# The first load of the output projection's weights in two unequal parts: 112 rows, then eight rows twice

## The chip, the core and the metric

The kernel runs on one core of one Trainium2 chip, alone. The metric is the device time of one execution in microseconds (us), the median of three runs. All data is float32.

## What is computed

One decoding step of a transformer block for a batch of two, one new position each: layer normalisation, attention over a cache of 8192 positions with 16 heads of 256, an output projection, a second layer normalisation and a gated feed-forward without a nonlinearity. Cut to what matters:

```python
B, D, H, Sk, Dh, F = 2, 448, 16, 8192, 256, 1792
n = layernorm(x)                                   # (B, 1, D)
q = (n @ wq) split into H heads of Dh
p = softmax(q . k_cache * Dh ** -0.5)              # k_cache, v_cache: (B, H, Sk, Dh)
o = p . v_cache                                    # (B, H, 1, Dh)
h = x + o (heads side by side) @ wo                # wo: (H * Dh, D)
m = layernorm(h)
out = h + ((m @ w_gate) * (m @ w_up)) @ w_down     # w_gate, w_up: (D, F); w_down: (F, D)
```

The two caches are 512 MiB of the 561 MB that the core reads.

## The kernel before, in words

The host lays every weight and every piece of the cache out as 128 rows, one for each partition of the on-chip memory, so that each load is a plain copy of 128 contiguous rows.

- All loads are issued from SyncE's queue (SP), in the order of the program, and run as one stream. The first is `wq_t` (line 107). Then come, for each of the 32 pairs of head and batch, one load of keys (`load_k`, line 98, one buffer in the pool `kbuf`) and one of values (`load_v`, line 103, two buffers in `vbuf`), each of 128 rows of 65,536 bytes.
- TensorE and VectorE share the scores (`scores`, lines 253 to 278), ScalarE makes the exponentials (line 324), VectorE multiplies and sums the values (lines 343 to 352). The key buffer comes free when the scores of a pair are done, so the load after it waits for VectorE's line 261 and TensorE's lines 269 and 275.
- After the 32 pairs the remaining weights reuse the same buffers. `wo_t`, the weights of the output projection, takes the key buffer; `gu_t` (gate and up) and `wd_t` (down) take the two value buffers. `wo_t` comes in three loads, cut by heads at `WO_CUTS = (8, 14)`: heads 0 to 7 (7168 columns, 28,672 bytes in each row), heads 8 to 13 and heads 14 and 15. Gate comes in two loads, up in three and down in six (lines 364 to 370), the later ones ever smaller.
- Line 395 (`project_out`) multiplies by `wo_t`, line 201 by `gu_t`, line 462 by `wd_t`. Line 476 and its partner on ScalarE copy the result, and line 477 stores two rows of it.
- The framework gives each load the next of eight completion semaphores (DMAHW0 to DMAHW7 in the rows further down). A load that takes a semaphore waits for the load that had it eight places earlier, unless the queue has waited for that already.

The function is one long stretch of code without loops on the chip; what the change touches are lines 357 to 359:

Of the kernel before, what the change touches and what calls it, by code (L numbers as in the profile page):

```python
# [15 lines left out]
P = 128  # L16
# [8 lines left out]
WO = 2 * D  # L25
# [34 lines left out]
def tile_decode_block(  # L60
# [24 lines left out]
    nc = tc.nc  # L85
# [270 lines left out]

    wo_t = kbuf.tile([P, H * WO], F32, tag="k", align_bytes=512, name="wo_t")
    for a, z in zip((0,) + WO_CUTS, WO_CUTS + (H,)):
        nc.sync.dma_start(wo_t[:, a * WO : z * WO], wo[:, a * WO : z * WO])
    gu_t = vbuf.tile([P, 2, WF], F32, tag="v", align_bytes=512, name="gu_t")  # L360
    wg_t, wu_t = gu_t[:, 0], gu_t[:, 1]
    wd_t = vbuf.tile([P, NF * D], F32, tag="v", align_bytes=512, name="wd_t")
# [51 lines left out]
    for m in range(DC + 1):  # L414
        at = min(m, DC - 1)
        rows = slice(0, P) if m < DC - 1 else slice((m - at) * HALF, (m - at + 1) * HALF)
# [128 lines left out]
```

## Time and profile before

| | |
|---|---|
| time, median of 3 runs | 1303.92 us (1303.78 to 1304.15) |
| profiled execution, first to last instruction (span) | 1302.1 us |
| difference between the two | 1.8 us |
| read from HBM | 561.19 MB, 431 GB/s over the span |
| VectorE busy | 1075.6 us (83%) |
| TensorE busy (matmul) | 340.6 us (26%) |
| the three loads of `wo_t` | 3584, 2688 and 896 KB, 16.5, 22.5 and 24.2 us from issue to landing |

A profile page of one execution gives, for each engine, its busy time; the span in 40 equal slices with the busy share of the 16 DMA engines and what they moved; the chain of work that ended last; and the costliest groups of instructions. A load's time to landing includes its place in the stream: the loads ahead of it have to go through first. KB are of 1024 bytes, MB and GB of 10^6 and 10^9.

### The profile page before, as it was taken

The numbers are of one execution on the slowest core, as the hardware profiler recorded it, in microseconds if no ns is written. First come the engines' busy times: TensorE is split into PE (matmuls) and PEld (weight loads), VectorE is DVE, ScalarE is ACT, GpSimd is POOL, SyncE is SP. The second block draws the span as 40 slices with busy tenths as digits, with TensorE's granted clock in tenths as the row PEclk, the third lists the DMA queues.
The fourth block names the chain that finished last, engine by engine and source line by source line (L and its number), as shares of the span: only waits on it lengthen the run. The fifth ranks groups of instructions, "written<-read, shape, count | busy, mean of one in ns | idle before, by whom it ended". The sixth has DMA issues, their size and how long they took to land.

```text
span 1302.1 us, 5034 instructions
## 1 busy us (share of the span) xinstructions
PE 340.6 (26%) x2114; PEld 103.4 (8%) x2114; DVE 1075.6 (83%) x381; ACT 80.4 (6%) x111; POOL 2.2 (0%) x15
## 2 busy tenths in 40 slices
PE   2422112232202223211322311322311232221247
PEld 0100000000000000000000000000000000000013
DVE  0499879969987998899799879979987996987773
ACT  1100000000000000000000000000000000000000
POOL 0000000000000000000000000000000000000000
PEclk9866566666556666556666556666656666656668
DMA  9999999999999999999999999999999999999998
GB/s 419 419 449 421 447 423 445 425 443 427 439 429 441 425 441 427 437 428 437 433 435 433 434 435 435 435 433 437 431 439 431 437 429 435 433 433 433 433 425 358
DMA packets 11401, 561.50 MB, mean 431 GB/s; under 512 B 1266, under 2 KB 1652, under 8 KB 2292
## 3 DMA queue, kind: packets, MB, share of 16 engines
q1 hardware_dynamic: 11380, 561.20, 99.6%
q8 instruction: 16, 0.26, 0.1%
q14 instruction: 5, 0.04, 0.0%
HBM read 561.19 MB, written 0.00 MB: 431 GB/s over the span
## 4 chain that ended last, share of the span: by engine, by line
DMA 73%; PE 17%; DVE 10%; issue 1%; SPq 0%; DVEq 0%; ACT 0%; ACTq 0%
DMA k<-in_kc_dram 67%; PE s L269 13%; DVE k L261 6%; DMA v<-in_vc_dram 4%; PE s L275 3%; DVE v L350 3%; DMA wd_t<-in_wd_dram 2%; DVE k L256 1%; PE acc_ps L462 0%; SPq L366 0%; SPq L107 0%; PE u_ps L462 0%; SPq L98 0%; DVEq L256 0%; ACT tail L184 0%
## 5 line engine op out<-in xcount | busy, mean ns | idle before, releaser
L269 PE MATMUL s<-k,q 128*32 128x512 f32 x1632 | 248.3, 773 | 892.5 <-DMA k<-in_kc_dram 892.5
L346 DVE TENSOR_TENSOR v<-v,p 128x16384 f32<-128x16384 f32 x19 | 327.3, 17226 | 81.2 <-DMA v<-in_vc_dram 61.2
L347 DVE TENSOR_REDUCE oacc<-v 128x8 f32<-128x16384 f32 x19 | 327.2, 17220 | 0.7
L350 DVE SCALAR_TENSOR_TENSOR v<-v,p 128x2048 f32<-128x2048 f32 x104 | 231.1, 2288 | 31.8 <-ACT p L324 21.9
L269 PEld LDWEIGHTS s<-k,q 128*32 128x32 f32 x1632 | 66.7, 138 | 1070.9 <-issue 1069.2
L324 ACT ACTIVATE p<-s,nm 128x2048 f32<-128x2048 f32 x32 | 63.0, 1967 | 1131.7 <-DVE nm L322 1131.7
L322 DVE TENSOR_REDUCE nm<-s 128x1 f32<-128x2048 f32 x32 | 73.1, 2285 | 33.8 <-PE s L275 33.8
L261 DVE SCALAR_TENSOR_TENSOR k<-k,qd 128x2048 f32<-128x2048 f32 (+1 forms) x52 | 93.4, 1817 | 1.4
L275 PE MATMUL s<-k,block 128*128 128x512 f32 x104 | 48.1, 605 | 18.1 <-DVE k L261 18.1
L256 DVE TENSOR_SCALAR k<-k,qd 128x2048 f32<-128x2048 f32 x13 | 16.7, 1286 | 29.2 <-DMA k<-in_kc_dram 27.0
L275 PEld LDWEIGHTS s<-k,block 128*128 128x128 f32 x104 | 18.7, 189 | 49.0 <-DVE k L261 33.5
L138 DVE TENSOR_REDUCE sum_h_x<-xT 128x2 f32<-128x6 f32 x1 | 0.2, 159 | 20.6 <-ACT xT L165 20.6
L395 PE MATMUL acc_ps<-wo_t,oT 128*2 128x448 f32 x64 | 8.8, 646 | 11.4 <-DMA wo_t<-in_wo_dram 11.2
L201 PE MATMUL q_ps<-wq_t,xr 128*32 128x512 f32 x64 | 9.6, 753 | 1.4 <-ACT xr L184 1.1
L350 DVE DVE_READ_ACCUMULATOR v<-v,p 128x1 f32 x104 | 8.6, 83 | 0.0
L201 PE MATMUL ff_ps<-gu_t,xr 128*32 128x512 f32 (+1 forms) x32 | 6.4, 913 | 0.6 <-ACT xr L184 0.6
L324 ACT ACTIVATION_READ_ACCUMULATOR p<-s,nm 128x1 f32 x32 | 6.2, 193 | 0.0
L148 PE MATMUL total_x<-sum_h_x,ones 128*128 128x2 f32 x2 | 0.6, 348 | 21.1 <-DVE sum_h_x L141 21.1
L442 DVE TENSOR_SCALAR ve<-var_h 128x1 f32<-128x1 f32 x1 | 0.2, 158 | 6.4 <-PE var_h L440 6.4
L476 DVE COPY tail<-acc_ps 2x112 f32<-2x112 f32 x1 | 0.3, 261 | 5.5 <-PE acc_ps L462 5.5
L245 ACT ACTIVATE q<-qT 128x128 f32<-128x128 f32 x16 | 4.8, 298 | 0.0
L201 PE MATMUL u_ps<-gu_t,xr 128*32 128x512 f32 (+1 forms) x32 | 3.6, 544 | 0.0
(103 smaller groups left out, 66.0 us busy)
## 6 DMA issues: line engine op xcount, KB each, us to landing
wq_t<-in_wq_dram SPq DMA_DIRECT2D x1, 7172.0 KB, 19.6
wo_t<-in_wo_dram SPq DMA_DIRECT2D x1, 3584.0 KB, 16.5
wo_t<-in_wo_dram SPq DMA_DIRECT2D x1, 2688.0 KB, 22.5
gu_t<-in_B_w_gate_dram SPq DMA_DIRECT2D x1, 1792.0 KB, 28.0
gu_t<-in_B_w_up_dram SPq DMA_DIRECT2D x1, 1792.0 KB, 34.5
gu_t<-in_B_w_gate_dram SPq DMA_DIRECT2D x1, 1344.0 KB, 30.7
wd_t<-in_wd_dram SPq DMA_DIRECT2D x1, 1120.0 KB, 16.8
wo_t<-in_wo_dram SPq DMA_DIRECT2D x1, 896.0 KB, 24.2
```

The lines of the kernel that those rows point to most:

```text
L201: nc.tensor.matmul(ps[32 * g : 32 * g + 32, : wide[g]], xs.rearrange("p b r -> p (b r)"), w[:, at : at + wide[g]], start=(c == 0), stop=(c ...
L245: nc.scalar.activation(q.rearrange("p c b r -> p (c b) r"), qT.rearrange("p k g j c b -> p (k g j) (c b)")[:, h, :, None] .to_broadcast([P ...
L256: nc.vector.tensor_scalar(upper[:, 0], upper[:, 0], qd[:, 0, i : i + 1], None, op0=ALU.mult)
L261: nc.vector.scalar_tensor_tensor(upper[:, 0, at], upper[:, o, at], qd[:, o, i : i + 1], upper[:, 0, at], op0=ALU.mult, op1=ALU.add,)
L269: nc.tensor.matmul(s[g * R : (g + 1) * R, at], q[:, c, i % B, :], kt[:, c, g, at], start=(c == 0), stop=(c == 1), skip_group_check=True,)
L275: nc.tensor.matmul(s[:, at], block, upper[:, 0, at], start=False, stop=True, skip_group_check=True,)
L322: nc.vector.tensor_reduce(nm[:, i : i + 1], s, axis=AX.X, op=ALU.max, negate=True)
L324: nc.scalar.activation(p, s, AF.Exp, bias=nm[:, i : i + 1], scale=1.0, accum_out=ls[:, i : i + 1])
L346: nc.vector.tensor_mul(v, v, p[:, None, :].to_broadcast([P, n, GK]))
L347: nc.vector.tensor_reduce(oacc[:, i, :n], v, axis=AX.X, op=ALU.add)
L350: nc.vector.scalar_tensor_tensor(v, v, 1.0, p, op0=ALU.mult, op1=ALU.mult, accum_out=oacc[:, i, o : o + 1])
L395: nc.tensor.matmul(acc_ps[32 * j : 32 * j + B, :], oT[:, h, c, :], wo_t[:, k * D : (k + 1) * D], start=(h < 2 and j > 0), stop=(h >= H - 2 ...
```

## The change

The first load of `wo_t`, 128 rows of 28,672 bytes, is issued as three loads: rows 0 to 111, rows 112 to 119 and rows 120 to 127, all of the same columns. The bytes and where they land are the same, and the other loads are as they were.

```diff
@@ -356,7 +356,9 @@
 
     wo_t = kbuf.tile([P, H * WO], F32, tag="k", align_bytes=512, name="wo_t")
     for a, z in zip((0,) + WO_CUTS, WO_CUTS + (H,)):
-        nc.sync.dma_start(wo_t[:, a * WO : z * WO], wo[:, a * WO : z * WO])
+        rows = (0, P - 2 * 8, P - 8, P) if a == 0 else (0, P)
+        for lo, hi in zip(rows, rows[1:]):
+            nc.sync.dma_start(wo_t[lo:hi, a * WO : z * WO], wo[lo:hi, a * WO : z * WO])
     gu_t = vbuf.tile([P, 2, WF], F32, tag="v", align_bytes=512, name="gu_t")
```

On SyncE's queue, this is the end of the program before the change: the three loads of `wo_t`, five of `gu_t`, six of `wd_t`, with the semaphores that each waits for (DMAHW are those of earlier loads, DVE and PE those of VectorE and TensorE).

```order
L359 DMA wo_t<-in_wo_dram 128x7168 [waits DMAHW7_49,DVE_49,PE_49]
L359 DMA wo_t<-in_wo_dram 128x5376
L359 DMA wo_t<-in_wo_dram 128x1792
L366 DMA gu_t<-in_B_w_gate_dram 128x3584 [waits DMAHW6_49]
L366 DMA gu_t<-in_B_w_gate_dram 128x2688
L366 DMA gu_t<-in_B_w_up_dram 128x3584
L366 DMA gu_t<-in_B_w_up_dram 128x1792
L366 DMA gu_t<-in_B_w_up_dram 128x896 [waits DMAHW0_49]
L366 DMA wd_t<-in_wd_dram 128x2240 [waits DMAHW1_49,DVE_49]
L366 DMA wd_t<-in_wd_dram 128x1792 [waits DMAHW2_49]
```

And the same stretch of the same queue after the change:

```order
L361 DMA wo_t<-in_wo_dram 112x7168 [waits DMAHW7_49,DVE_49,PE_49]
L361 DMA wo_t<-in_wo_dram 8x7168 x2
L361 DMA wo_t<-in_wo_dram 128x5376
L361 DMA wo_t<-in_wo_dram 128x1792
L368 DMA gu_t<-in_B_w_gate_dram 128x3584 [waits DMAHW6_49]
L368 DMA gu_t<-in_B_w_gate_dram 128x2688
L368 DMA gu_t<-in_B_w_up_dram 128x3584 [waits DMAHW0_49]
L368 DMA gu_t<-in_B_w_up_dram 128x1792 [waits DMAHW1_49]
L368 DMA gu_t<-in_B_w_up_dram 128x896 [waits DMAHW2_49]
L368 DMA wd_t<-in_wd_dram 128x2240 [waits DMAHW3_49,DVE_49]
L368 DMA wd_t<-in_wd_dram 128x1792 [waits DMAHW4_49]
```

Two loads are added, so every later load takes a semaphore two places on. The wait for the last load of values (DMAHW0) now stands at the first load of up and not at the third, and the second and third load of up wait for the first two parts of the split load.

On TensorE's queue, the two places of the output projection that wait for the first and the second load of `wo_t`, before:

```order
L395 MATMUL acc_ps<-wo_t,oT 2x448 [waits DMAHW1_49]
L395 MATMUL acc_ps<-wo_t,oT 2x448 x15
L395 MATMUL acc_ps<-wo_t,oT 2x448 [waits DMAHW2_49]
L395 MATMUL acc_ps<-wo_t,oT 2x448 x11
L395 MATMUL acc_ps<-wo_t,oT 2x448 [waits DMAHW3_49]
```

After the change:

```order
L397 MATMUL acc_ps<-wo_t,oT 2x448 [waits DMAHW3_49,DMAHW2_49,DMAHW1_49]
L397 MATMUL acc_ps<-wo_t,oT 2x448 x15
L397 MATMUL acc_ps<-wo_t,oT 2x448 [waits DMAHW4_49]
L397 MATMUL acc_ps<-wo_t,oT 2x448 x11
L397 MATMUL acc_ps<-wo_t,oT 2x448 [waits DMAHW5_49]
```

The first matmul of the projection now waits for all three parts; the rest is in the same order.

## The prediction

> **What bounds the kernel now.** I read the page first: the slices of the DMA engines, the queues, and the chain that ended last.
>
> ```profile
> span 1302.1 us, 5034 instructions
> DMA  9999999999999999999999999999999999999998
> q1 hardware_dynamic: 11380, 561.20, 99.6%
> q8 instruction: 16, 0.26, 0.1%
> DMA 73%; PE 17%; DVE 10%; issue 1%; SPq 0%; DVEq 0%; ACT 0%; ACTq 0%
> ```
>
> All 16 DMA engines are busy in every slice but the last, and the chain is mostly DMA. So the kernel ends when the stream of loads ends, plus a tail; what a change does to the stream decides. The chain in order of time shows the tail.
>
> ```profile
> 1259.63 17.80 DVE v L350 x16
> ...
> 1278.29 19.73 DMA wd_t<-in_wd_dram
> ...
> 1299.74 0.26 ACT tail L184
> ```
>
> The timeline shows how tightly the tail follows the last load of `wd_t`, and when the loads of the last part are issued (start, duration, what).
>
> ```profile
> 1251.54 1.28 SPq L359 DMA_DIRECT2D wo_t<-in_wo_dram  x3
> 1253.80 6.14 SPq L366 DMA_DIRECT2D gu_t<-in_B_w_up_dram  x3
> 1277.44 11.23 SPq L366 DMA_DIRECT2D wd_t<-in_wd_dram  x6
> 1299.24 0.09 PEld L462 LDWEIGHTS u_ps<-wd_t,hmT 128*2 128x2 f32 x2 [0.20 <-DMA wd_t<-in_wd_dram]
> 1300.02 0.33 SPq L477 DMA_DIRECT2D out_dram<-tail  x1
> ```
>
> The last piece of `wd_t` has landed at about 1299.2 us, when TensorE is let go, and the rest takes 1302.1 - 1299.2 = 2.9 us whatever came before. So one microsecond on the last landing is one microsecond on the time.
>
> The 16 engines don't end together. Busy times in short stretches (start and end, five engines, clock, DMA share, GB/s) of the steady part and the last microseconds:
>
> ```profile
> 100.00:1200.00 1100.00, 261.33 (x1557) 75.19 (x1557) 963.05 (x295) 60.52 (x71) 0.00 (x0) 0.63 1.00 434
> 1295.00:1295.90 0.90, 0.90 (x39) 0.87 (x41) 0.00 (x0) 0.00 (x0) 0.00 (x0) 1.00 0.94 366
> 1296.50:1297.00 0.50, 0.50 (x24) 0.50 (x28) 0.00 (x0) 0.00 (x0) 0.00 (x0) 1.00 0.54 220
> 1297.50:1298.00 0.50, 0.00 (x0) 0.00 (x0) 0.00 (x0) 0.00 (x0) 0.00 (x0) 1.00 0.51 186
> 1298.00:1298.50 0.50, 0.44 (x20) 0.44 (x24) 0.00 (x0) 0.00 (x0) 0.00 (x0) 1.00 0.44 149
> 1298.50:1299.00 0.50, 0.50 (x26) 0.21 (x16) 0.00 (x0) 0.00 (x0) 0.00 (x0) 1.00 0.08 27
> ```
>
> At 1296.5 us the share has fallen to 0.54, which is 0.54 x 16 = 8.6 engines; it is 7.0 engines at 1298.0 to 1298.5, and nearly none after. So some seven engines are done by 1296.5, and the other nine 1.5 to 2.7 us later. What makes them differ I can only guess: the queue of instructions above brings 0.26 MB in 16 pieces of 16 KB, each of which holds one engine for 0.6 us at the rate below, and nothing evens that out. The early ones can't help the late ones, since each load gives every engine its share in advance.
>
> **The change part by part.** How rows go to engines is read from packet counts. This is the answer for the 0.4 us in which the two rows of the result are stored.
>
> ```profile
> DMA packets 4, 0.00 MB, mean 9 GB/s; under 512 B 2, under 2 KB 4, under 8 KB 4
> ```
>
> Two packets of data and two tiny ones, which mark the end. The page's queue q1 has 11380 packets: 79 loads of 128 rows with 16 marks each, 79 x 144 = 11376, and these 4. So each row is one packet, a load of 128 rows runs on 16 engines with eight rows each, and a transfer of two rows on two engines. From this I take it that a load of eight rows runs on eight engines, one row each, and one of 112 on sixteen, seven rows each. [...] If both eight-row loads take the same eight engines, these get 7 + 1 + 1 = 9 rows and the other eight get 7, in place of 8.
>
> *A row at an engine's own rate.* 434 GB/s over 16 engines is 27.1 GB/s; 28,672 bytes take 1.06 us. The unsplit load takes 8 x 1.06 = 8.46 us.
>
> *What a load of eight rows takes.* No load of the profile reaches fewer than 128 partitions, so I bound it. Low end: the eight engines each run at their own rate, 1.06 us. High end: the eight partitions together take in no more than eight of the 128 ever do in this profile, 434 / 16 = 27.1 GB/s, so eight rows take 8 x 1.06 = 8.46 us. In every load here 16 engines share 128 partitions, so the profile can't tell whether 27.1 GB/s belongs to an engine or to the place it writes to. I take the middle, (1.06 + 8.46) / 2 = 4.76 us, which means that about four or five engines share one way in.
>
> [...]
>
> *The sum on the eight engines.* Before 8.46 us. After 7 x 1.06 + 2 x 4.76 = 16.92 us, which is 8.46 us more. The other eight engines have one row less, -1.06 us.
>
> *What of it reaches the end.* Each engine works through its own list in order, so a delay stays with it to the end, less the slack it had. Nine engines are late and the split burdens eight, leaving only eight others; so at least one of the nine is among the burdened. The eighth or ninth from the end finishes where the count falls from 8.2 to 7.0 engines, at about 1298.0, a slack of 1299.2 - 1298.0 = 1.2 us at most, and none at least. I take 0.6. Then the last landing moves by 8.46 - 0.6 = 7.9 us.
>
> *Issues.* Two more instructions on SyncE's queue:
>
> ```profile
> L359 SPq DMA_DIRECT2D wo_t<-in_wo_dram x3: 328/424/425, 1251.5 to 1252.4; - x3
> SPq L366 <- DMA v<-in_vc_dram: 4.9, 1, 4.9
> wo_t<-in_wo_dram SPq DMA_DIRECT2D x1, 3584.0 KB, 16.5
> ```
>
> At 0.42 us each, every load behind is issued 0.85 us later. That costs nothing: the last load of values isn't through before 1259.6 (VectorE waited for it, above), and the first load of `wo_t` keeps the engines until 1251.5 + 16.5 = 1268.0.
>
> *Waits.* The first load of up, issued at 1253.8 before, now waits for the last load of values, so until about 1259.6 (the third did before, 4.9 us in the row above); behind it stand only the other loads of up and those of `wd_t`, which wait for VectorE until 1277.4 in any case. The loads of `wo_t` and gate queued ahead are 3584 + 2688 + 896 + 1792 + 1344 KB = 10.6 MB, 24 us at 434 GB/s from about 1257; the first load of up has its turn at about 1281. The second and third of up wait for parts of `wo_t`, landed by 1268 (1276 with the delay), and have their turn after 1285. Price nothing; if the cover were gone it would be what the queue is then empty. TensorE's first matmul of `wo_t` waits for all three parts, at 1268.1 before and up to 8 us later in this forecast. The projection, gate and up then move with the stream, as the loads that they wait for do; they have the same distance to the last load as before.
>
> *In all.* Span 1302.1 + 7.9 = 1310.0. The median lies 1303.9 - 1302.1 = 1.8 us above the span, so 1311.8 us, 0.6% slower.
>
> **The rivals.**
>
> *Only engines count: no slower.* An eight-row load takes 1.06 us. The burdened engines have one row more, +1.06, less a slack of 0 to 1.2: the end moves by -0.1 to +1.06, say +0.5, so 1304.4. For it: every engine ran at the same rate through the steady part (share 1.00 at 434 GB/s), as if each were its own limit. Against it: that rate was never seen at any other sharing of partitions. Point of decision: an eight-row load that lands within some 2.5 us on an idle engine. Chance 0.28.
>
> *The shift is a gain.* Same price, but the engines with nine rows are just the early ones and one more that is nearly early, and all the late ones have seven. Then the late end moves by up to -1.06: 1302.9, 0.08% faster. For it: early and late are about half and half (8.6 engines). Against: nine don't fit into eight. Chance 0.10.
>
> *It does not do what it says.* The eight-row loads are cut over all 16 engines, and nothing moves but 0.85 us of issue: 1303.9. Against it stand the two packets of two rows. Chance 0.05.
>
> *The 112 rows collide too.* With seven rows to an engine, engines no longer keep to groups of eight partitions of their own; if half of the seven rows are shared with one other engine, they take 7 x 1.06 / 2 = 3.7 us more, on top of 7.9: 1303.9 + 11.6 = 1315.5. It needs the same limit as the forecast. Chance 0.13.
>
> *The high end.* Each eight-row load takes 8.46 us: 7.4 + 16.9 - 8.46 - 0.6 = 15.3 us, 1319.2. Chance 0.05.
>
> **How the numbers follow.** The forecast has 0.37, with a range of its own: four engines to one way in and the whole slack give 7.40 + 2 x 4.23 - 8.46 - 1.2 = 6.2 us, 1310.1; five and no slack give 7.40 + 2 x 5.29 - 8.46 = 9.5 us, 1313.4. 0.02 is left for something faster that I don't see. A measurement of this kernel can tell about 0.2%, 2.6 us, from no change: slower than 1306.5 are the forecast, the collision and the high end, 0.55; within are the next three, 0.28 + 0.10 + 0.05 = 0.43; faster 0.02. The range goes from 1303.0, which takes in the rivals without a limit but the last of the gain, to 1315.6, which takes in the collision; outside are the high end and half of the gain.
>
> **What would show it.** In the changed profile: the time to landing of the eight-row loads and of the second load of `wo_t` (22.5 us before) would be longer by 6 us or more; the DMA share would fall to about half right after the first loads of gate or up have ended on the free engines, some 8 us ahead of the last landing, in place of 2.7; the wait of TensorE for `wo_t` would grow by about 8 us; and the last stretch would show about eight busy engines for that long. What would prove it wrong: the wait for `wo_t` at 1268 us moves by a microsecond or less, and the share in the last microseconds falls as before.

## The result and the profile after

The changed kernel takes 1318.62 us (median of four runs, 1318.57 to 1320.68) against 1303.95; the ratio is 1.0117, with a 95% interval of 1.0102 to 1.0131. It is 14.7 us slower, where 7.9 were forecast (1311.8) and the range ended at 1315.6. The profile is of the run of 1320.68 us, two above the median; it is 16.7 us longer than the kernel before.

The page of the changed kernel, its DMA rows, its queue and the second load of `wo_t` with its time to landing:

```profile
span 1318.9 us, 5037 instructions
DMA  9999999999999999999999999999999999999997
GB/s 414 444 415 442 441 421 440 432 433 436 423 440 439 425 438 439 428 434 439 431 430 442 432 429 440 433 431 434 437 433 432 435 437 424 442 440 417 445 231 331
q1 hardware_dynamic: 11396, 561.20, 99.5%
wo_t<-in_wo_dram SPq DMA_DIRECT2D x1, 2688.0 KB, 38.4
```

The engines are as busy as before, but the slice of 33 us that begins at 1253 us moves 231 GB/s. Busy is not the same as moving bytes: a packet counts from its start to its end however slowly it goes (a share of 1.04 goes with 156 GB/s below). The packet count settles how rows are dealt out: 78 loads of 128 rows with 16 marks (11232), 112 rows with 16 (128), twice eight rows with eight (32) and four for the result make 11396. So each eight-row load did run on eight engines, as the prediction took it.

In stretches of 5 us (the last two columns are DMA share and GB/s), first before, then after:

```profile
1255.00:1260.00 5.00, 2.69 (x12) 1.52 (x12) 1.03 (x5) 1.55 (x5) 0.00 (x0) 0.50 0.88 382
1260.00:1265.00 5.00, 0.00 (x0) 0.00 (x0) 5.00 (x5) 0.00 (x0) 0.00 (x0) 0.50 0.98 421
1265.00:1270.00 5.00, 1.88 (x12) 0.40 (x16) 5.00 (x5) 0.00 (x0) 0.00 (x0) 0.50 0.98 423
1270.00:1275.00 5.00, 3.38 (x32) 0.70 (x28) 5.00 (x5) 0.00 (x0) 0.00 (x0) 0.87 0.98 412
1275.00:1280.00 5.00, 3.90 (x41) 0.83 (x29) 3.37 (x7) 0.00 (x0) 0.00 (x0) 1.00 1.01 432
1280.00:1285.00 5.00, 4.12 (x30) 2.63 (x34) 1.09 (x7) 0.94 (x4) 0.00 (x0) 0.65 1.01 431
```

```profile
1255.00:1260.00 5.00, 2.81 (x12) 1.68 (x12) 0.65 (x4) 1.67 (x5) 0.00 (x0) 0.50 0.99 233
1260.00:1265.00 5.00, 0.00 (x0) 0.00 (x0) 2.22 (x1) 0.00 (x0) 0.00 (x0) 0.50 0.93 206
1265.00:1270.00 5.00, 0.00 (x0) 0.00 (x0) 5.00 (x7) 0.00 (x0) 0.00 (x0) 0.50 1.02 224
1270.00:1275.00 5.00, 0.00 (x0) 0.00 (x0) 5.00 (x5) 0.00 (x0) 0.00 (x0) 0.50 1.04 156
1275.00:1280.00 5.00, 0.00 (x0) 0.00 (x0) 5.00 (x5) 0.00 (x0) 0.00 (x0) 0.50 0.99 185
1280.00:1285.00 5.00, 0.00 (x0) 0.00 (x0) 0.74 (x3) 0.00 (x0) 0.00 (x0) 0.50 0.86 267
1285.00:1290.00 5.00, 4.71 (x28) 1.02 (x32) 0.00 (x0) 0.00 (x0) 0.00 (x0) 0.50 0.99 419
```

Most of the loss lies between 1255 and 1285 us, and after it the stream runs at 419 GB/s as before. In these 30 us 12.5 MB were moved before (the six rates times 5 us) and 6.4 MB after; the 6.1 MB missing are 14.5 us at 424 GB/s, of the 16.7 us by which this run is longer. The stretch has two halves. Up to 1270 us it is mainly the 112 rows, beside the end of the last load of values: three lines of about 221 GB/s, half the usual rate, at which 112 x 28,672 bytes take 14.5 us (an estimate, since the loads overlap). From 1270 to 1285 us come the last of the 112 rows, the eight-row loads and, on the engines that have ended them, the second load of `wo_t`, at 156 to 267 GB/s.

The other two microseconds lie at the end. There the engines stop less evenly than before: from 1312 to 1315 us only two or three of the 16 are still at work (0.18 x 16 = 2.9, 0.11 x 16 = 1.8).

```profile
1311.00:1312.00 1.00, 1.00 (x24) 0.57 (x28) 0.00 (x0) 0.18 (x1) 0.00 (x0) 1.00 0.61 223
1312.00:1313.00 1.00, 0.90 (x34) 0.62 (x22) 0.00 (x0) 0.00 (x0) 0.00 (x0) 1.00 0.18 73
1314.00:1315.00 1.00, 0.34 (x16) 0.29 (x16) 0.00 (x0) 0.00 (x0) 0.00 (x0) 1.00 0.11 39
```

The timeline after, SyncE's issues, TensorE's first matmul of `wo_t` and its last load of weights:

```profile
1262.78 20.07 SPq L368 DMA_DIRECT2D gu_t<-in_B_w_up_dram  x3
1285.29 8.77 PE L397 MATMUL acc_ps<-wo_t,oT 128*2 128x448 f32 x58 [26.59 <-DMA wo_t<-in_wo_dram]
1315.89 0.09 PEld L464 LDWEIGHTS u_ps<-wd_t,hmT 128*2 128x2 f32 x2 [0.22 <-DMA wd_t<-in_wd_dram]
```

TensorE gets its first weights of the projection at 1285.3, 17 us later than at 1268.1; the last landing is at 1315.9, 16.7 us later in this run, and the tail behind it takes 3.0 us, as the 2.9 before. The first load of up waits for the last load of values and was issued at 1262.8, at 1259.6 before: so that load, which the change doesn't touch, was slowed by the loads that began beside it.

### The profile page after: what moved, and what is told of

Its sections match the earlier page's. It is cut to its first block, busy times and chain, and to the rows that moved or that the text cites. A ratio compares the mean times of both kernels' runs of the same rounds, so it can differ in the third digit from the quotient of the medians.

```text
span 1318.9 us, 5037 instructions
## 1 busy us (share of the span) xinstructions
PE 343.7 (26%) x2114; PEld 103.9 (8%) x2114; DVE 1075.5 (82%) x381; ACT 80.4 (6%) x111; POOL 2.2 (0%) x15
## 3 DMA queue, kind: packets, MB, share of 16 engines
q1 hardware_dynamic: 11396, 561.20, 99.5%
## 4 chain that ended last, share of the span: by engine, by line
DMA 73%; PE 17%; DVE 9%; issue 1%; SPq 0%; DVEq 0%; ACT 0%; ACTq 0%
DMA k<-in_kc_dram 68%; PE s L269 13%; DVE k L261 6%; PE s L275 4%; DMA wo_t<-in_wo_dram 3%; DVE v L350 2%; DMA wd_t<-in_wd_dram 2%; DVE k L256 1%; SPq L361 0%; PE acc_ps L464 0%; SPq L107 0%; PE u_ps L464 0%; DVEq L256 0%; ACT tail L184 0%; PE ff_ps L464 0%
## 5 line engine op out<-in xcount | busy, mean ns | idle before, releaser
L256 DVE TENSOR_SCALAR k<-k,qd 128x2048 f32<-128x2048 f32 x13 | 16.7, 1286 | 29.1 <-DMA k<-in_kc_dram 27.0
L397 PE MATMUL acc_ps<-wo_t,oT 128*2 128x448 f32 x64 | 10.1, 741 | 26.9 <-DMA wo_t<-in_wo_dram 26.6
L478 DVE COPY tail<-acc_ps 2x112 f32<-2x112 f32 x1 | 0.3, 263 | 5.5 <-PE acc_ps L464 5.5
## 6 DMA issues: line engine op xcount, KB each, us to landing
wo_t<-in_wo_dram SPq DMA_DIRECT2D x1, 2688.0 KB, 38.4
```

The lines of the kernel that those rows point to most:

```text
L256: nc.vector.tensor_scalar(upper[:, 0], upper[:, 0], qd[:, 0, i : i + 1], None, op0=ALU.mult)
L397: nc.tensor.matmul(acc_ps[32 * j : 32 * j + B, :], oT[:, h, c, :], wo_t[:, k * D : (k + 1) * D], start=(h < 2 and j > 0), stop=(h >= H - 2 ...
```

## The experiments

The costs below are against the kernel before as it ran beside each experiment (1303.8 to 1304.1 us). After the result I held theory A: the slow part is the way into the on-chip memory, where rows that go to adjacent partitions hold each other up. The rivals: B, each partition by itself takes no more than its 3.4 GB/s (an estimate, 434 over 128 partitions); C, only an engine's rate counts and the time is lost in the new waits; D, the loss is on the reading side, in the order of the rows in memory.

**Each load by itself on an idle stream** (e1_alone). Behind the store of the result:

```diff
     nc.sync.dma_start(out.rearrange("b s d -> (b s) d"), y)
+    nc.sync.dma_start(wo_t[0:128, : 8 * WO], wo[0:128, : 8 * WO])
...
+    nc.sync.dma_start(wo_t[0:8, : 8 * WO], wo[0:8, : 8 * WO])
+    nc.sync.dma_start(wo_t[0:16:2, : 8 * WO], wo[0:16:2, : 8 * WO])
+    nc.sync.dma_start(wo_t[0:32:4, : 8 * WO], wo[0:32:4, : 8 * WO])
...
```

> Nine further loads of the first eight heads' columns stand after the store of the result, each waiting for the one before it, so each runs on an idle stream: 128 rows, 112, 64, 16, 8 adjacent, 8 with a step of 2, 8 with a step of 4, 8 with a step of 16, and 128 again. The result is not touched by them; only the times between their issues are read, and the whole runs some 50 us longer. [...] Theory B, each partition by itself takes in no more than its 3.4 GB/s: 8.5 us for every one of them, whatever the rows and the step. Theory C, only engines count and the time in the changed kernel came from its new waits: 8.5, 7.4, 4.2, 1.06, and 1.06 for all loads of eight rows.

SyncE's timeline of that run; each load overwrites rows of the one before and waits for it, so the step from one start to the next is one load. In order: 128 rows, 112, 64, 16, 8 adjacent, 8 with a step of 2, of 4, of 16, and 128 again.

```profile
1300.65 0.36 SPq L478 DMA_DIRECT2D wo_t<-in_wo_dram  x1
1311.55 0.33 SPq L479 DMA_DIRECT2D wo_t<-in_wo_dram  x1
1325.63 0.56 SPq L480 DMA_DIRECT2D wo_t<-in_wo_dram  x1
1337.49 0.33 SPq L481 DMA_DIRECT2D wo_t<-in_wo_dram  x1
1343.82 0.28 SPq L482 DMA_DIRECT2D wo_t<-in_wo_dram  x1
1349.29 0.72 SPq L483 DMA_DIRECT2D wo_t<-in_wo_dram  x1
1353.71 0.63 SPq L484 DMA_DIRECT2D wo_t<-in_wo_dram  x1
1357.15 0.58 SPq L485 DMA_DIRECT2D wo_t<-in_wo_dram  x1
1361.48 0.36 SPq L486 DMA_DIRECT2D wo_t<-in_wo_dram  x1
```

Each load was timed once. 128 rows take 10.90 us, of which 8.46 are the bytes at 434 GB/s; I take the other 2.44 as the same for all, which is not shown: issuing a load with a step alone takes 0.58 to 0.72 us, and 0.28 the eight adjacent rows (second column above).

| load | start to start, us | less 2.44 | at the engines' rate |
|---|---|---|---|
| 128 rows | 10.90 | 8.46 | 8.46 |
| 112 rows | 14.08 | 11.6 | 7.4 |
| 64 rows | 11.86 | 9.4 | 4.2 |
| 16 rows | 6.33 | 3.9 | 1.06 |
| 8 adjacent | 5.47 | 3.0 | 1.06 |
| 8, step 2 | 4.42 | 2.0 | 1.06 |
| 8, step 4 | 3.44 | 1.0 | 1.06 |
| 8, step 16 | 4.33 | 1.9 | 1.06 |

Theories B and C fall: the four loads of eight rows have the same bytes, on eight engines each (the nine loads add 592 packets, 11,972 against 11,380 before, which are their rows and a mark from each engine), and take 1.0 to 3.0 us by where they go. Adjacent rows are the slowest, as theory A has it, but distance alone does not order the rest: with a step of 16 the rows lie furthest apart, and they take 1.9 us, about the 2.0 of a step of 2 and 0.9 more than with a step of 4. Why is not shown. The 0.9 us are less firm than the gap between adjacent and spread rows, since the same load taken again in the next experiment differs by 0.3 to 0.5 us.

The 112 rows take longer than 128, 14.08 against 10.90 us, with fewer bytes and one row less for each engine. The runs don't show why: no view here shows which engine writes which rows, or in what order.

**Writing side or reading side** (e5_crossed). Above, rows lay in memory as they lay on the partitions. Here they are crossed, and then loads are put close behind each other:

```diff
+    nc.sync.dma_start(wo_t[0:8, 0 : 8 * WO], wo[0:8, 0 : 8 * WO])
+    nc.sync.dma_start(wo_t[0:8, 0 : 8 * WO], wo[0:32:4, 0 : 8 * WO])
+    nc.sync.dma_start(wo_t[0:32:4, 0 : 8 * WO], wo[0:8, 0 : 8 * WO])
+    nc.sync.dma_start(wo_t[0:32:4, 0 : 8 * WO], wo[0:32:4, 0 : 8 * WO])
...
```

> Again loads after the store of the result, which is not touched; here rows come from other rows of wo than those they are written to, so what the further loads bring is of no use, and only times between issues are read. First four loads of eight rows: adjacent partitions from adjacent rows of memory, adjacent partitions from every fourth row, every fourth partition from adjacent rows, every fourth from every fourth. Theory A (ways into the on-chip memory): about 5.5, 5.5, 3.4 and 3.4 us between issues. Theory D (the order in which memory is read): 5.5, 3.4, 5.5 and 3.4. Then 128 rows of 21,504 bytes alone, and the same right behind eight adjacent rows, right behind eight rows with a step of 4, and last 112, 8 and 8 rows together on an idle stream. If an engine that waits for its way holds up only itself: 8.8 us, 11.9 (3.1 more), 9.8 (1 more), and 20.3 for the three (11.7 + 3.1 + 3.1 + 2.4). If it holds up other engines too: clearly over 11.9 and over 20.3.

SyncE's timeline again. L478 to L481 are the four crossed loads, L483 the 128 rows alone, L485 and L486 the pair with adjacent rows, L488 and L489 the pair with a step of 4, L491 to L493 the three parts of the change; the others separate them.

```profile
1300.58 0.29 SPq L478 DMA_DIRECT2D wo_t<-in_wo_dram  x1
1306.52 0.27 SPq L479 DMA_DIRECT2D wo_t<-in_wo_dram  x1
1312.09 0.74 SPq L480 DMA_DIRECT2D wo_t<-in_wo_dram  x1
1315.84 0.63 SPq L481 DMA_DIRECT2D wo_t<-in_wo_dram  x1
1319.58 0.37 SPq L482 DMA_DIRECT2D wo_t<-in_wo_dram  x1
1324.05 0.35 SPq L483 DMA_DIRECT2D wo_t<-in_wo_dram  x1
1332.80 0.33 SPq L484 DMA_DIRECT2D wo_t<-in_wo_dram  x1
1337.20 0.29 SPq L485 DMA_DIRECT2D wo_t<-in_wo_dram  x1
...
1349.54 0.33 SPq L487 DMA_DIRECT2D wo_t<-in_wo_dram  x1
1353.78 0.67 SPq L488 DMA_DIRECT2D wo_t<-in_wo_dram  x1
...
1364.17 0.33 SPq L490 DMA_DIRECT2D wo_t<-in_wo_dram  x1
1368.51 0.33 SPq L491 DMA_DIRECT2D wo_t<-in_wo_dram  x1
...
1389.47 0.35 SPq L494 DMA_DIRECT2D wo_t<-in_wo_dram  x1
```

The four take 5.94, 5.57, 3.75 and 3.74 us: the partitions decide, and the order in memory does not. Theory D falls. (The first and the last of them took 5.47 and 3.44 us in the experiment before.) The 128 rows alone take 8.75 us, behind eight adjacent rows 12.34 (3.6 more, 3.1 expected), behind eight with a step of 4 10.39 (1.6 more, 1 expected). The three parts of the change together take 20.96 us, close to the 20.3 that they add up to. So on an idle stream the change costs 20.96 - 10.90 = 10.1 us. I read these times as an engine that waits holding up little beside itself, but they can't show it, since the eight engines with the additional rows end last either way. The trace can. Here are the first four microseconds of the 128 rows alone, behind adjacent rows and behind rows with a step of 4:

```profile
1325.00:1329.00 4.00, 0.00 (x0) 0.00 (x0) 0.00 (x0) 0.00 (x0) 0.00 (x0) 0.50 1.05 382
1338.00:1342.00 4.00, 0.00 (x0) 0.00 (x0) 0.00 (x0) 0.00 (x0) 0.00 (x0) 0.50 1.10 186
1355.00:1359.00 4.00, 0.00 (x0) 0.00 (x0) 0.00 (x0) 0.00 (x0) 0.00 (x0) 0.50 0.90 326
```

Eight undisturbed engines would move half of 382 GB/s, 191, and the eight adjacent rows are another 57 (229,376 bytes in 4 us), 248 in all. All 16 together move 186. In the packets of the trace the other eight engines' first rows of 21,504 bytes take 2.1 to 2.4 us, and 0.9 to 1.7 in the load alone. So adjacent rows slow the engines without eight-row loads on an idle stream too.

**The waits alone** (e2_columns):

```diff
+        cols = (0, 6272, 6720, 7168) if a == 0 else (a * WO, z * WO)
+        for lo, hi in zip(cols, cols[1:]):
+            nc.sync.dma_start(wo_t[:, lo:hi], wo[:, lo:hi])
```

> The first load of wo_t is split into three by columns (6272, 448 and 448 of 7168), each of all 128 rows. Number and places of the loads, semaphores and waits are those of the changed kernel; how rows lie on partitions is that of the kernel before. Theory C (waits and issues): about 1318.6 us as in the changed kernel. Theories A and B (what a load of few rows reaches): about 1304 us, within 0.5 of before.

1304.09 us, ratio 1.000 (0.999 to 1.0009). The two additional loads, their issue and all the moved semaphores cost nothing. That settles C for the stream as well.

**No eight-row loads, and nothing uneven** (e3_112_16 and e4_64_64). In the changed loop:

```diff
-        rows = (0, P - 2 * 8, P - 8, P) if a == 0 else (0, P)
+        rows = (0, 112, P) if a == 0 else (0, P)
```

> Rows 0 to 111 and 112 to 127, two loads, so that all engines have eight rows again and none has nine. [...] Theory B: 8.5 us for each load, 1312. If only the eight-row loads had cost something, as my forecast had it: 1304 to 1308. Theory C: 1304 to 1311.

```diff
-        rows = (0, P - 2 * 8, P - 8, P) if a == 0 else (0, P)
+        rows = (0, 64, P) if a == 0 else (0, P)
```

> Rows 0 to 63 and 64 to 127, two loads, four rows for each engine in each, so nothing is uneven. [...] Theory B: 8.5 us each as well, 1312. Theory C, and the forecast's reading that an engine's load matters: 1304.

1317.32 us (ratio 1.0101, 1.0086 to 1.0117) and 1316.72 (1.0096, 1.0081 to 1.0111). In both every engine has its eight rows, as before the change (11,396 packets in each run, 16 more than before for the 16 marks of one more load), and yet they lose 13.2 and 12.6 us, nearly all that the change loses. So nine rows against seven is at most the last 1.5 to 2 us of what the change costs; the rest comes with loads that aren't of 128 rows. Both lie above all that was expected (1312 by theory B).

**The parts by themselves in the stream** (e6_extra_adjacent, e7_extra_step4, e8_extra_112). The kernel before, with loads added that nothing reads:

```diff
-    wd_t = vbuf.tile([P, NF * D], F32, tag="v", align_bytes=512, name="wd_t")
+    wd_t = vbuf.tile([P, NF * D + 8 * WO], F32, tag="v", align_bytes=512, name="wd_t")
...
+    for rows in (slice(112, 120), slice(120, 128)):
+        nc.sync.dma_start(wd_t[rows, NF * D :], wo[rows, : 8 * WO])
```

> The kernel before with two more loads ahead of those of wd_t: rows 112 to 119 and 120 to 127 of the first heads of wo, into a part of the buffer that nothing reads. So the two eight-row loads come in the stream as in the change, but without the 112 rows. Price by the runs on an idle stream 3.1 us each: 6.2, less a slack under 1 us, since three of the engines that took eight-row loads were late ones: 1309 to 1310.5. If waiting engines hold up the others: 1311 or more. By the forecast on record, 4.76 us each: 1312 to 1313.5. If only engines count: 1305 to 1306.

With `slice(0, 32, 4), slice(64, 96, 4)` in the same place:

> [...] Theory A: an engine's own rate, 1.06 us each, 2.1 less a slack under 1: 1305 to 1306. If eight-row loads are slow whatever partitions they reach: as the adjacent ones, 1309 or more.

With `slice(0, 112)` alone:

> The kernel before with one more load of 112 rows of 28,672 bytes ahead of those of wd_t, into a part of the buffer that nothing reads. At the engines' own rate 7.4 us: 1311.5. By its time on an idle stream 11.7: 1315.8. By what the profile of the changed kernel shows for its 112 rows in the stream, 14 to 15, and something after it: 1318 to 1320.

They cost 9.7 us (1313.67, ratio 1.0074, 1.0059 to 1.0089), 4.8 us (1308.84, 1.0035, 1.0023 to 1.0048) and 17.5 us (1321.56, 1.0135, 1.012 to 1.015). Adjacent rows cost twice what spread ones do here too, with the same bytes on eight engines for each load (11,412 packets in both runs). But each costs 3 to 6 us more than on an idle stream, where two times 3.0, two times 1.0 and 11.6 were measured. The rates of the run with the two adjacent loads:

```profile
1285.00:1290.00 5.00, 5.00 (x34) 1.83 (x30) 0.32 (x2) 0.23 (x1) 0.00 (x0) 0.68 1.13 348
1290.00:1295.00 5.00, 2.15 (x20) 0.27 (x10) 0.00 (x0) 0.46 (x1) 0.00 (x0) 1.00 0.97 163
1295.00:1300.00 5.00, 3.03 (x12) 0.78 (x12) 0.76 (x2) 0.18 (x1) 0.00 (x0) 0.50 0.94 220
```

At 163 GB/s all 16 engines together do the work of six, though only eight have eight-row loads. My expectation that a waiting engine holds up only itself is wrong here as well.

**Engines in step** (e9_before_drained and e10_after_drained). By the packets of the traces the engines begin the first load of `wo_t` up to 3.3 us apart in the stream before the change, and the same load on an idle stream within 0.7 us. A load of one column into the last tile of values makes SyncE wait until all have ended; the first load of `wo_t` is then issued at 1260.34 us and not at 1251.54:

```diff
         vt = load_v(b, h)
+        if i == NQ - 1:
+            nc.sync.dma_start(vt[:, 0, :1], vc[b, h][:, :1])
```

> The kernel before with a load of one column (512 bytes) into the last tile of values, which must wait until that tile has landed; so the loads of wo_t are issued only when all engines have ended, and the 16 engines start them in step. It is the base for the run with the same and the split load. The late engines lose the way from issue to first byte, about 1.3 us; the early ones lose what they were ahead: 1305 to 1306.5.

> The changed kernel (112, 8 and 8 rows) with the same drain ahead of it. On an idle stream the three loads took 21.0 us where the unsplit one took 10.9: 10.1 more. In the stream the change cost 14.7. If the other 4 to 5 us come from engines that are out of step when the short loads begin: 10 to 11 us over the drained kernel before. If they come from the loads that follow, or from anything else that the drain leaves: 14 to 15 over it.

1308.34 us (ratio to the kernel before 1.0034, 1.0022 to 1.0047) without the split and 1320.04 (1.0125, 1.011 to 1.014) with it. The drain itself cost 4.5 us where 1 to 2.5 were expected (1305 to 1306.5), which stays open. On top of it the split costs 11.7 us, between the 10 to 11 of the one case and the 14 of the other, nearer to the first. So of the 4.6 us that the change loses in the stream beyond an idle one, some 3 go with the drain. It was to put the engines in step, and it also leaves no load of values under way beside the 112 rows (118 GB/s from 1255 to 1260 us, 382 before); which of the two it is was not separated. The remaining 1.6 us are open.

## Why the prediction was wrong

- *What bounds the kernel* held: the end moved with the last landing, and the tail stayed at 3 us.
- *Eight rows on eight engines, a row a packet* held, by the packet count (11396).
- *Issues and waits at nothing* held: 1304.09 us with both and without uneven rows.
- *112 rows at 7 x 1.06 = 7.40 us* is the step that failed. It took each engine's own rate for granted there, while the very next term doubted it for eight rows. The load takes 11.6 us on an idle stream, about 14.5 in the changed kernel, and alone it makes the kernel 17.5 us slower (e8_extra_112). The rival "the 112 rows collide too" had named this, with 3.7 us and a chance of 0.13; 4.2 us on an idle stream is its size, and some 7 in the stream. Why these rows take so long is open.
- *An eight-row load at 4.76 us* was too dear for one by itself (3.0 us on an idle stream). That four or five engines share one way in, as I read it from this figure, no run shows. Two such loads cost 9.7 us in the stream, near the 9.5 that I had put on the eight engines. That agreement is by chance, since the cost doesn't stay on these engines:
- *The other eight engines have one row less, -1.06 us* was wrong too. From 1270 to 1285 us the whole stream runs at 156 to 267 GB/s, where it had 412 to 432 before.
- *Only engines count, no slower* (0.28) and *a gain* (0.10) fall: eight adjacent rows take 3.0 us and not 1.06, and only the step of 4 keeps an engine's own rate (1.0). *It does not do what it says* (0.05) falls by the packet count.
- *The high end* (0.05) comes within a microsecond of the measured time with 1319.2, but by chance: it has 8.46 us for each eight-row load, and two of them cost 9.7.
- *What would show it*: the second load of `wo_t` was to land 6 us later or more, and landed 16 later (38.4 us after its issue, 22.5 before). A DMA share of one half for 8 us was expected, and isn't there: the share stays near 1 and the rate falls.

## What to carry to other kernels

The loads of fewer than 128 partitions could not be costed here by their bytes or by rows per engine: 112 rows took longer than 128 (14.08 against 10.90 us), and eight rows took 1.0 to 3.0 us by the partitions that they were written to. When a DMA stream looks fully busy, read GB/s beside the share: here a share of 1.04 went with 156 GB/s. To even out engines by a microsecond, don't cut a load by rows, which cost 12.6 to 14.7 us here; a cut by columns was free, and none of the versions tried here is faster than the kernel before.

## What the runs showed of the hardware

- Eight rows of 28,672 bytes on eight engines take 3.0, 2.0, 1.0 or 1.9 us beyond the 2.44 taken as fixed, for steps of 1, 2, 4 and 16 partitions (each timed once; two of them, repeated, differ by up to 0.5 us).
- The source's order doesn't matter: 5.57 against 5.94 us with rows spread or adjacent in memory, both into adjacent partitions.
- 112 rows take 14.08 us on an idle stream, and 128 rows 10.90.
- Adjacent rows slow engines that have no part in them: 186 GB/s for 382 on an idle stream, 163 in the running one. In a running stream the added loads cost 3 to 6 us more than on an idle one.
